# Mixing the next group's preparation into a recurrence: a change of five parts to a chunked RWKV-7 and FFN kernel

## The chip, the cores and the metric

One core of a Trainium2 chip runs the whole kernel. The metric is the device time of one execution in microseconds (us), and less is better. Most executions agree closely; some fall into a slower state with a lower granted TensorE clock. A run that is over 1.5% above the fastest of its kernel is called slow, and fast runs are compared with fast runs only.

Names: PE is TensorE's matmul, PEld its weight load, DVE is VectorE, ACT is ScalarE, POOL is GpSimd, SP is SyncE, which issues most DMAs. L235 is line 235 of the kernel in question, so the same instruction has different lines in different kernels. "Granted" time is time multiplied by the granted clock (1.0 is full, 0.5 half): the full-clock time that TensorE was given.

## The reference

```python
# 4 batches x 8 heads, 768 steps, head_dim 40; all fp32
for t in range(S):
    y[:, :, t] = einsum('bhd,bhde->bhe', rt, state)
    Sa = einsum('bhde,bhe->bhd', state, at)
    state = state * wt[:, :, None, :] - einsum('bhd,bhe->bhde', Sa, bt) \
            + einsum('bhd,bhe->bhde', vt, kt)
x = y.transpose(0, 2, 1, 3).reshape(3072, 320)
h = x @ w_in                        # 320 x 2048, given as float64
g = h * clip(h + 3, 0, 6) / 6
out = g @ w_out                     # 2048 x 320, given as float64
```

The kernel handles the 768 steps in six groups of 128. Within a group the steps become matrix products with a 128x128 lower-triangular system per head. "Preparation" makes all that does not need the state (decay products, scores, the system's blocks); "inversion" inverts the 32x32 diagonal blocks on VectorE; the "recurrence" carries the state through the group and yields 128 tokens per batch; the FFN runs on those tokens. The weights arrive as 64-bit floats, which the kernel takes as pairs of 32-bit words and rounds to fp32 itself, 36 tiles of 128x256 or 128x320.

## The kernel before

`ps_any` gives one of three PSUM banks, `ps_acc` one of two.

```python
def rounded(dst, n, loads):                       # one tile of weights
    raw = tmp.tile([P, DM, 2], U32, name="raw", tag="yg", bufs=2)   # shares yg's slots
    buf = ffn.tile([P, 3, DM], U32, name="parts", tag="gt")
    ...                                           # DMAs on ScalarE's queue; 9 VectorE operations:
    nc.vector.tensor_scalar(x, hi, 20, 0x7FF, ALU.logical_shift_right, ALU.bitwise_and)
    nc.vector.tensor_scalar(e, x, 896.0, 1151.0, ALU.max, ALU.min)
    ...
    nc.gpsimd.tensor_tensor(out=dst, in0=dst, in1=e, op=ALU.add)

def masked(x, s, products):                       # one half (64 rows) of the heads
    o = ps_any([P, 4, P])
    for n, (lhs, rhs) in enumerate(products):     # contraction over 40 rows
        nc.tensor.matmul(out=o[:, n, :], lhsT=lhs, rhs=rhs, start=True, stop=True)
    nc.vector.copy_predicated(out=x[:, 4 * s:4 * s + 4, :], mask=mask4, data=o[:])

def invert(fc):
    ...
    for s in range(1, L):
        nc.vector.tensor_tensor(out=prod, in0=tcol[:, 0:s, 0:s]..., in1=..., op=ALU.mult)
        nc.vector.tensor_reduce(out=tcol[:, s, 0:s], in_=prod, axis=AX.X, op=ALU.add, negate=True)
    ...                                           # then four transposes into tinv

for g in range(NG):                               # the order of a group
    os_ = [prepare(g, q, fc) for q in range(B)]
    invert(fc)
    for q, o in enumerate(os_):
        off_diagonal(q, o)                        # the first to use tinv
    for q, o in enumerate(os_):
        step(q, o)
        outputs(g, q, o, xts[-1])
    if g == 0:
        load_weights()
    else:
        for i, x in enumerate(last):              # FFN of the group before, 256 tokens at a time
            feed_forward(g - 1, i * NB, x)
```

## Time and profile before

The median of four runs was 1623.59 us (1617.91 to 1660.72, the highest one slow). The profiled execution took 1636.3 us at a mean granted clock of 0.742.

| stretch of the kernel before | length, us | granted clock |
|---|---|---|
| preparation 0 | 69 | |
| inversion 0, nothing beside it | 50 | 0.50 |
| recurrence 0, weights, preparation 1 | 197 | 0.59 |
| inversion 1, nothing beside it | 65 | |
| recurrence 1, most of the rounding, preparation 2 | 301 | 0.69 |
| inversion 2 to 5, FFN beside it | 54 each | |
| recurrence and preparation, FFN between | 175, 178, 178 | 0.78 to 0.80 |
| recurrence 5 and the last FFN | 207 | |

A stretch here ends at the first use of an inverse or at the transposes that begin an inversion. From group 2 on the kernel repeats itself every 232 us with TensorE busy; before that it is VectorE's inversions and the weights that hold everything. The prediction below shows and reads the lines of this profile.

### The profile page before, as it was taken

How to read it: one execution, taken by the hardware profiler on the slowest of the kernel's cores; microseconds unless marked ns; L12 is line 12 of the kernel's file. 1: busy time of each engine (PE TensorE's matmuls, PEld its weight loads, DVE VectorE, ACT ScalarE, POOL GpSimd, SP SyncE). 2: the span in 40 equal slices, each digit the busy share in tenths (PEclk: the TensorE clock that was granted, in tenths of full speed). 3: DMA queues.
4: the chain of work that ended last, by engine and by line, in shares of the span. 5: the costliest groups of instructions: out<-in, count | busy, mean ns of one | idle time of the engine just before them, and what ended most of it. 6: DMA issues, size and time to landing. Idle time of an engine off the chain costs nothing.

```text
span 1636.3 us, 21883 instructions
## 1 busy us (share of the span) xinstructions
PE 1360.5 (83%) x8880; PEld 1107.9 (68%) x8880; DVE 775.7 (47%) x1289; ACT 314.3 (19%) x793; POOL 164.4 (10%) x407
## 2 busy tenths in 40 slices
PE   6709987506159999979999989998899999799998
PEld 5608876506048777758877668877577777588765
DVE  6681148897751223691234862245942236912111
ACT  2302112201001112312122221123121123121111
POOL 4100012211110001100011000011000011000000
PEclk6557555556556698788795997786987877876899
DMA  4201022212200012101111101012001121000000
GB/s 63 34 0 22 18 50 57 66 30 55 72 29 18 9 23 41 25 8 22 27 34 29 21 13 25 18 36 41 9 14 22 27 40 25 8 6 8 12 9 12
DMA packets 172949, 44.16 MB, mean 27 GB/s; under 512 B 155952, under 2 KB 168240, under 8 KB 172848
## 3 DMA queue, kind: packets, MB, share of 16 engines
q1 hardware_dynamic: 167184, 32.27, 10.7%
q10 hardware_dynamic: 5664, 10.49, 2.2%
q8 instruction: 70, 1.15, 0.3%
q14 instruction: 31, 0.25, 0.1%
HBM read 34.08 MB, written 3.93 MB: 23 GB/s over the span
## 4 chain that ended last, share of the span: by engine, by line
PE 64%; DVE 27%; ACT 4%; issue 3%; POOL 1%; DMA 0%; ACTq 0%; DVEq 0%; SPq 0%; POOLq 0%
PE h L494 9%; DVE prod L346 8%; PE any L235 8%; PE o L513 7%; PE any L226 7%; DVE tcol L350 6%; PE acc L414 5%; PE acc L407 4%; PE acc L459 4%; PE any L426 4%; PE acc L394 4%; PE any L331 3%; PE h L501 3%; DVE tinv L354 3%; PE any L365 2%
## 5 line engine op out<-in xcount | busy, mean ns | idle before, releaser
L494 PE MATMUL h<-xt,win 128*128 128x256 f32 x768 | 231.9, 453 | 38.5 <-DVE gt L508 30.3
L513 PE MATMUL o<-wout,gt 128*128 128x320 f32 x768 | 232.9, 457 | 10.5 <-DVE gt L508 9.3
L494 PEld LDWEIGHTS h<-xt,win 128*128 128x128 f32 x768 | 166.8, 229 | 75.1 <-DVE gt L508 39.2
L513 PEld LDWEIGHTS o<-wout,gt 128*128 128x128 f32 x768 | 147.8, 198 | 83.9 <-issue 16.5
L236 DVE COPY_PREDICATED score<-mask,any 128x512 f32<-128x512 int32 x144 | 100.5, 722 | 134.5 <-PE any L235 133.9
L508 DVE SCALAR_TENSOR_TENSOR gt<-gt,h 128x512 f32<-128x512 f32 x96 | 63.0, 683 | 175.6 <-ACT gt L506 175.5
L346 DVE TENSOR_TENSOR prod<-tcol,fb 128x1 f32<-128x1 f32 (+30 forms) x186 | 137.1, 737 | 5.0
L432 DVE TENSOR_TENSOR ssum<-any,state 128x160 f32<-128x160 f32 x24 | 7.8, 325 | 273.4 <-PE any L426 273.4
L506 ACT ACTIVATE gt<-h,three 128x512 f32<-128x512 f32 x96 | 61.3, 684 | 243.3 <-PE h L501 242.8
L394 PE MATMUL acc<-state,at 40*128 40x40 f32 x384 | 63.8, 333 | 52.7 <-DVE yg L470 52.7
L501 PE MATMUL h<-xt,win 64*128 64x256 f32 x384 | 75.2, 452 | 29.2 <-POOL win L180 29.2
L394 PEld LDWEIGHTS acc<-state,at 40*128 40x128 f32 x384 | 57.7, 241 | 60.1 <-DVE yg L470 54.5
L365 PE MATMUL any<-tinv,ft 128*96 128x96 f32 x384 | 39.3, 271 | 69.5 <-DVE tinv L354 69.5
L350 DVE TENSOR_REDUCE tcol<-prod 128x1 f32<-128x1 f32 (+30 forms) x186 | 93.5, 502 | 5.0
L414 PEld LDWEIGHTS acc<-U,ft 64*32 64x32 f32 (+2 forms) x1152 | 71.5, 151 | 33.3 <-issue 14.6
L419 ACT ACTIVATE U<-acc 32x320 f32<-32x320 f32 x96 | 41.1, 428 | 273.2 <-PE acc L407 183.5
L235 PE MATMUL any<-at,kt 40*128 40x128 f32 x384 | 75.7, 356 | 19.5 <-ACT ft L320 12.0
L235 PE MATMUL any<-cross 40*128 40x128 f32 x768 | 89.1, 329 | 0.0
L365 PEld LDWEIGHTS any<-tinv,ft 128*96 128x96 f32 x384 | 38.4, 186 | 72.4 <-issue 66.6
L235 PEld LDWEIGHTS any<-cross 40*128 40x128 f32 x768 | 83.8, 227 | 5.2 <-issue 5.2
L331 PEld LDWEIGHTS any<-VN,score 128*128 128x128 f32 x384 | 78.2, 302 | 10.7 <-DVE prod L346 5.5
L414 PE MATMUL acc<-U,ft 64*32 64x40 f32 (+2 forms) x1152 | 82.2, 249 | 3.9 <-ACT U L419 3.9
(101 smaller groups left out, 1899.0 us busy)
## 6 DMA issues: line engine op xcount, KB each, us to landing
raw<-in_moe_w_out_dram ACTq DMA_DIRECT2D x16, 320.0 KB
WN<-in_w_dram SPq DMA_DIRECT2D x24, 160.0 KB
VN<-in_v_dram SPq DMA_DIRECT2D x96, 40.0 KB
AN<-in_a_dram SPq DMA_DIRECT2D x24, 160.0 KB
KN<-in_k_dram SPq DMA_DIRECT2D x24, 160.0 KB
BN<-in_b_dram SPq DMA_DIRECT2D x24, 160.0 KB
RN<-in_r_dram SPq DMA_DIRECT2D x96, 40.0 KB
out_dram<-ob SPq DMA_DIRECT2D x24, 160.0 KB
```

Source lines behind the costliest of these rows:

```text
L226: nc.tensor.transpose(out=o[:, n, :], in_=x[:, 2 * n:2 * n + 2, :].rearrange("p s e -> p (s e)"), identity=ident[:])
L235: nc.tensor.matmul(out=o[:, n, :], lhsT=lhs, rhs=rhs, start=True, stop=True)
L236: nc.vector.copy_predicated(out=x[:, 4 * s:4 * s + 4, :], mask=mask4, data=o[:])
L331: nc.tensor.matmul(out=ev[:, cross(h), :], lhsT=E[:, h % 2 * 4 + h // 2, :], rhs=VN[:, cross(h), 0:D], start=True, stop=True)
L346: nc.vector.tensor_tensor(out=prod, in0=tcol[:, 0:s, 0:s].rearrange("p u t -> p t u"), in1=_ap(fb[:], s * L, [[0, s], [1, s]]), op=ALU.mult,)
L350: nc.vector.tensor_reduce(out=tcol[:, s, 0:s], in_=prod, axis=AX.X, op=ALU.add, negate=True)
L365: nc.tensor.matmul(out=wp[0:LW, pr, :], lhsT=ft[:, 4 * s + pr, :], rhs=tinv[:, q * H + 2 * pr + s, L:P], start=True, stop=True)
L394: nc.tensor.matmul(out=rp[s][:, pr, :], lhsT=o["at"][rows, pr, :], rhs=st[rows, pr, 0:D], start=True, stop=True)
L414: nc.tensor.matmul(out=up[cr, cross(h), :], lhsT=o["F"][0:c * L, h % 2 * 4 + h // 2, (c - 1) * L:c * L], rhs=U[0:c * L, cross(h), 0:D], st ...
L494: nc.tensor.matmul(out=hp[half][:, i, :], lhsT=win[:, kt_, j * P:(j + 1) * P], rhs=xt[:, kt_, :], start=(kt_ == 0 and i == 0), stop=False)
L501: nc.tensor.matmul(out=hp[half][:, i, :], lhsT=win2[rows, (j0 + i) * P:(j0 + i + 1) * P], rhs=xt[rows, 2, :], start=False, stop=(i == 1))
L513: nc.tensor.matmul(out=op[:], lhsT=gt[:, j, i * P:(i + 1) * P], rhs=wout[:, j, :], start=(j == 0), stop=(j == NJ - 1))
```

## The change

The intent has five parts. *Order*: the preparation of group g+1 is issued between the four recurrences of group g, and the FFN of 128 tokens gets the lowest priority ("behind"), to fill what is left. *Row halves paired*: products that use 40 of the 128 rows come alternately from the upper and the lower half of the array, each half with a PSUM bank of its own, so that two can run together. *Inversion in place*: 30 rank-1 updates, two VectorE operations each, without reductions. *Weights*: fewer VectorE operations, two of them moved to GpSimd, and the loads start at once. *FFN by 128 tokens* instead of 256.

```diff
+BEHIND = 1 << 20
 ...
-        buf = ffn.tile([P, 3, DM], U32, name="parts", tag="gt")
+        buf = ffn.tile([P, 3, DM], U32, name="parts", bufs=1)
-            nc.scalar.dma_start(out=raw[rows, 0:n, :],
+            nc.sync.dma_start(out=raw[rows, 0:n, :],
 ...
         nc.vector.tensor_scalar(x, hi, 20, 0x7FF, ALU.logical_shift_right, ALU.bitwise_and)
-        nc.vector.tensor_scalar(e, x, 896.0, 1151.0, ALU.max, ALU.min)
 ...     (eight VectorE operations and one on GpSimd removed; five on VectorE, three on GpSimd now:)
+        nc.gpsimd.tensor_scalar(ef, x, 896.0, 1151.0, ALU.max, ALU.min)
+        nc.vector.tensor_scalar(x, ef, -896.0, 8388608.0, ALU.add, ALU.mult)
         nc.vector.scalar_tensor_tensor(x, hi, 0x80000000, x, ALU.bitwise_and, ALU.bitwise_or)
+        nc.vector.tensor_scalar(m, hi, 0xFFFFF, 0x4B000000, ALU.bitwise_and, ALU.bitwise_or)
+        nc.gpsimd.tensor_scalar(ef, mf, -7.0 * 2 ** 20, 2.0 ** -20, ALU.add, ALU.mult)
+        nc.vector.scalar_tensor_tensor(mf, lo, 2.0 ** -52, ef, ALU.mult, ALU.add)
+        nc.gpsimd.tensor_tensor(out=dst, in0=mf, in1=xf, op=ALU.mult)
 ...
-    def masked(x, s, products):
-        o = ps_any([P, 4, P])
-        for n, (lhs, rhs) in enumerate(products):
-            nc.tensor.matmul(out=o[:, n, :], lhsT=lhs, rhs=rhs, start=True, stop=True)
-        nc.vector.copy_predicated(out=x[:, 4 * s:4 * s + 4, :], mask=mask4, data=o[:])
+    def masked(x, lhs, rhs):
+        o = [ps_any([P, NPR, P]) for _ in range(2)]
+        for n in range(NPR):
+            for s in range(2):
+                rows = slice(SLOT * s, SLOT * s + D)
+                nc.tensor.matmul(out=o[s][:, n, :], lhsT=lhs[rows, n, :], rhs=rhs[rows, n, :],
+                                 start=True, stop=True)
+        for s in range(2):
+            nc.vector.copy_predicated(out=x[:, 4 * s:4 * s + 4, :], mask=mask4, data=o[s][:])
 ...     (the same for at with bt, at with state, and the sums into sn and y)
+        for k in range(1, L - 1):               # inversion in place
+            nc.vector.tensor_tensor(out=pv, in0=_ap(x[:], (k + 1) * L + k, [[L, n], [0, k]]),
+                                    in1=_ap(x[:], k * L, [[0, n], [1, k]]), op=ALU.mult)
+            nc.vector.tensor_tensor(out=rest, in0=rest, in1=pv, op=ALU.add)
 ...
+    os_ = prepared(0)
+    with behind():
+        load_weights()
+    for g in range(NG):
+        def recur(q):
+            step(q, os_[q])
+            xt = outputs(g, q, os_[q])
+            with behind():
+                feed_forward(g, q, xt)
+        if g + 1 < NG:
+            os_ = prepared(g + 1, recur)        # recur(q) ahead of each prepare(g + 1, q)
+        else:
+            for q in range(B):
+                recur(q)
```

## The prediction

> **What bounds the kernel now.** I read the page first, then one period of the steady state cut into its stages, then the longest waits, then instructions in order of time.
>
> ```profile
> PE 1360.5 (83%) x8880; PEld 1107.9 (68%) x8880; DVE 775.7 (47%) x1289; ACT 314.3 (19%) x793; POOL 164.4 (10%) x407
> ...
> PE   6709987506159999979999989998899999799998
> ...
> PEclk6557555556556698788795997786987877876899
> ```
>
> TensorE (PE) is busy in nine tenths or more of most slices from the fourteenth on, at a clock that is granted only in part. Before that are two holes (slice 3, slices 9 to 13). The stretches below are, in columns, start:end and length, busy time of PE, weight load, VectorE, ScalarE and GpSimd with counts, then the granted clock.
>
> ```profile
> 316.00:490.00 174.00, 59.78 (x465) 52.38 (x466) 131.68 (x312) 13.38 (x27) 27.75 (x36) 0.53 0.17 48
> ...
> 912.00:965.00 53.00, 43.20 (x177) 30.55 (x175) 51.03 (x74) 6.38 (x11) 0.00 (x0) 0.90 0.03 9
> 965.00:1063.00 98.00, 97.70 (x920) 81.62 (x922) 21.48 (x43) 20.61 (x42) 6.99 (x24) 0.81 0.11 21
> 1063.00:1144.00 81.00, 75.79 (x388) 62.39 (x385) 36.05 (x44) 24.95 (x79) 13.78 (x36) 0.75 0.21 38
> ```
>
> The last three make one period of 232 us (a group): inversion on VectorE with FFN matmuls beside it, the four recurrences, the next group's preparation. Only in the inversion is VectorE full. The first stretch is group 1 with the rounding of the weights, where VectorE is full and PE a third busy. The waits say the same (who waited for whom, total us, times, longest):
>
> ```profile
> PE any L365 <- DVE tinv L354: 69.5, 6, 44.5
> PE acc L394 <- DVE yg L470: 52.7, 1, 52.7
> ```
>
> L365 waits for an inversion with no FFN to put beside it. L394 stands behind outputs whose yg shares its two slots with the raw weights.
>
> Is PE at its limit in the steady state? I took the time between starts of consecutive matmuls in the trace: at full clock 109 ns for 128 columns with 128 weight columns, 216 for 256, 269 for 320, 112 for 40 columns behind 128 weight columns, 56 for 128 columns in 64-column tiles; at half clock twice that. Counts times these, for the run: FFN h 768 x 216 = 166, its half-row part 384 x 108 = 42, o 768 x 269 = 207: 414 us. The rest: transposes 816 x 109 = 89; K=40 products (L310, L235) 1536 x about 97 = 150; L331, L394, L407 1152 x 112 = 129; L365 384 x 85 = 33; L414 1152 x 36 = 42; L426 768 x 49 = 38; L459 and L466 1152 x 56 = 64: 545 us. In all 959 us of full clock. The mean clock of 0.742 over 1636 us grants 1214. In the recurrence stage (965 to 1063) the work fills what the clock grants; so in the steady state TensorE work and its clock are the bound, and before 490 us it is the weights and inversions.
>
> **What the Trainium skill says.** (1) "TensorE: Matmul & The Clock Gate", Part 1: the clock is either half or full, by recent activity, in windows of about 3.4 us. The trace agrees: only spacings of 109 or 213 ns. Windows that hold mostly transposes and 40-column matmuls are followed by half clock; those that stream FFN by full clock (the end, from 1538 us, is at 1.00). (2) The same page, Part 3: matmuls on different row groups run together. It agrees: half-row matmuls start in pairs 7 ns apart, and eight of them take less than a third of the time of sixteen full ones:
>
> ```profile
> 1572.61 3.72 PE L494 MATMUL h<-xt,win 128*128 128x256 f32 x16 [0.22 <-DVE gt L508]
> 1576.26 1.13 PE L501 MATMUL h<-xt,win 64*128 64x256 f32 x8
> ```
>
> (3) "LDWEIGHTS" in the same page: the load goes by weight columns, 128/1.2 = 107 ns. The 112 ns of 40-column matmuls agree, so an FFN matmul of 128 columns is as long as its weight load. (4) "VectorE: DVE Perf Modes", on the errata: fp32 tensor_tensor takes (N+151)/0.96 ns. The reduce of 961 agrees (1.16 us against 1.158); the product that reads with a stride does not:
>
> ```profile
> 953.56 1.79 DVE L346 TENSOR_TENSOR prod<-tcol,fb 128x961 f32<-128x961 f32 x1
> ...
> 955.85 1.16 DVE L350 TENSOR_REDUCE tcol<-prod 128x31 f32<-128x961 f32 x1
> ...
> 957.51 7.73 DVE L354 STREAM_TRANSPOSE tinv<-tcol 32x1024 f32<-32x1024 f32 x4
> ```
>
> **The change part by part** (PE in us of full clock).
>
> *Row halves paired.* 1536 K=40 products go from about 97 to 56 ns: -63. L394 112 to 58: -21. L426, its halves of columns now alternating, 49 to 29: -15. L466, now four tiles at once, 56 to 28: -11. Sum -110, so 849 remain: 435 recurrent, 414 FFN.
>
> *FFN by 128 tokens.* h becomes 1536 x 109 = 167 instead of 166; o is unchanged; ACT and DVE handle the same 96 tiles of 512. Nothing saved by itself; it gives smaller pieces for gaps, with no slack left for weight loads.
>
> *Inversion.* Two passes of sum k(31-k) = 4960 elements: 9920/0.96 = 10.3 us, plus 60 instructions x 157 ns = 9.4, plus 40 ns between them (as now) 2.4: 22.1. Two transposes of 2.05 us: 4.1. The select about 1.5 and two copies in a row on ACT or POOL about 2.6 (estimates from POOL's 0.40 us for 256 elements and ACT's 0.60 for 512). About 31, with some FFN tiles between 34, against 53.7 now (911.6 to 965.3). VectorE saves about 25 us a group. On the path this counts in full only for the first inversion, which has nothing beside it; later it shortens the stage where PE starves for gt (some 10 us a group).
>
> *Weights.* VectorE per tile of 320: now nine operations, 3.7 us; afterwards 0.33+0.33+0.49+0.32+0.49 = 2.0. Two operations move to POOL. With one parts buffer, tiles stay serial: 2.0 less the 0.32 that overlaps, two POOL operations of about 0.55 (estimate), the last of 0.86, and handovers: about 4.3 us, as now (4.7). So 36 tiles take about 155 us, but can start at the first inversion, not after group 0, and leave VectorE half free.
>
> *Order.* The recurrence of g and preparation of g+1 are mixed and FFN fills gaps. The sum of PE work is the same; its use and clock change. Each change of tile shape costs about 95 ns at full clock (640 changes now); mixing may double them, some +60 us.
>
> The time line: preparation 0 to 64 (68 now, less pairing), inversion to 95. Stage of recurrence 0 and preparation 1: PE work 72 at the clock of such stages (0.58 now) and 85% use: 147 us, to 242; VectorE 55 + 65 of weights fits. Inversion 1 to 276, FFN just begun (12 us of it). Work left: 849 - 28 - 72 - 12 = 737, plus 45 of mode changes beyond those in today's rate: 782. Today's rate in the period is 161/232 = 0.69 (clock 0.82, use 0.85). FFN is now 43% of PE work and becomes 49%, spread: stretches with half FFN show 0.9 now, those with a third 0.75. I take clock 0.88 and use 0.94, 0.83: 942 us, to 1218, and about 10 for the last copy and store: 1228. I chose 1225.
>
> **The rivals.** *Clock stays low.* If small pieces of FFN don't lift the clock (0.75, use 0.92), 782/0.69 = 1133 and 1420. For it: preparation runs at 0.75 with a third FFN. Against: the end at 1.00. *Waits vanish better than thought*, clock 0.95 and use 0.95, few mode changes: 737/0.90 = 819, 1105. *Weights hold up again.* raw still shares slots with yg, and its DMAs now stand in SyncE's queue before the inputs: a hole like 409 to 466 would add 40 to 60: 1275. *VectorE becomes the bound*: per group about 88 us, against 142 of PE: no. *Pairing is done already*: the scheduler pairs some (L310 means 95, not 111), which I counted; if bank waits undo it, +60.
>
> **Range and chances.** Clock and use together from 0.74 to 0.92 give 1340 to 1135; so 1120 to 1335. Slower than 1592 needs a rate below 0.60, worse than today's period with less work: faster 0.96, same 0.03, slower 0.01.
>
> **What would show it.** Right: L365 first near 97; one wait for tinv; first FFN near 255; periods of 170 to 190 us; PEclk mostly 0.8 to 1; L310 and L235 in pairs, with PE's group of L235 halved; the 60 inversion operations near 22 us. Wrong: a hole after 95 longer than 20 us; gt waits; clock of 0.7 in mixed stages; a tail of FFN alone longer than 60 us.

## The result

The change brought 1411.36 us (median of four runs, 1406.3 to 1413.78), against 1623.59 before. Ratios in this document are the mean time of one kernel's fast runs over that of the other's of the same rounds, so they are not quite the ratio of the medians; here 0.8699, with a 95% interval of 0.866 to 0.8738. One hundredth of the ratio is about 16 us. So the kernel became faster, as expected, but 186 us slower than the predicted 1225 and above the top of the range, 1335.

The page of the kernel after, with TensorE's and VectorE's totals, then TensorE's busy tenths and its granted clock in 40 slices of the span:

```profile
span 1411.0 us, 24203 instructions
...
PE 1214.1 (86%) x10032; PEld 1041.7 (74%) x10032; DVE 582.2 (41%) x1113; ACT 327.2 (23%) x805; POOL 248.1 (18%) x503
...
PE   5732725999999998999999999898998999999998
...
PEclk9555656669957899886877759976999989899999
```

TensorE is full from the eighth slice on instead of the thirteenth, and VectorE's busy time fell from 775.7 to 582.2 us. But two holes remain at the start (slices 3 to 4 and 6), and the clock wavers between 0.5 and 0.9 until slice 28. The mean clock rose from 0.742 to 0.805. Span times clock is 1214 granted us before and 1136 after: 78 us less, where the prediction took 110 us of full clock out of the matmuls alone. One caution for every mean clock below: the trace's clock record begins late (at 12 us before, 34 us after), and the profile counts the time until then as full clock, although matmuls of 128 columns start 213 ns apart there, which is half clock. Counted as half, the means are 0.739 and 0.793.

Stretches of the kernel after, in the same columns as the prediction's (start:end and length, then busy time and count of PE, weight load, VectorE, ScalarE, GpSimd, then granted clock and DMA): preparation 0, inversion 0, the stage of recurrence 0 with preparation 1, inversion 1, all that follows, and from it the mixed stage of group 1 and the end.

```profile
0.00:86.00 86.00, 53.25 (x272) 47.23 (x272) 53.15 (x87) 21.81 (x72) 47.40 (x96) 0.72 0.39 74
86.00:131.00 45.00, 3.82 (x16) 3.56 (x16) 38.56 (x105) 2.39 (x3) 22.49 (x29) 0.50 0.17 53
131.00:334.00 203.00, 148.37 (x1262) 130.17 (x1263) 90.24 (x178) 42.62 (x116) 77.20 (x121) 0.66 0.24 53
334.00:366.00 32.00, 27.00 (x186) 22.72 (x185) 25.98 (x67) 6.04 (x10) 3.48 (x4) 0.99 0.03 11
366.00:1411.00 1045.00, 981.70 (x8300) 837.99 (x8299) 374.30 (x678) 254.31 (x606) 97.52 (x255) 0.85 0.12 23
...
366.00:508.00 142.00, 138.16 (x1270) 120.31 (x1270) 53.96 (x79) 42.44 (x115) 21.05 (x60) 0.77 0.21 34
...
1212.00:1405.00 193.00, 179.42 (x1305) 149.16 (x1306) 27.21 (x44) 29.00 (x50) 0.00 (x0) 0.97 0.03 12
```

Here the miss can be split. The prediction's time line has inversion 1 done at 276 and 952 us after it (942 and 10 for the last store). The trace has 366 and 1045. **So 90 us were lost at the start and 93 us afterwards**; together 183, the whole difference to 1228. Two things are to be explained.

What TensorE waited for in the kernel after (who for whom, total us, times, longest):

```profile
PE any L375 <- POOL tinv L367: 46.0, 4, 41.5
PE acc L403 <- DVE yg L479: 44.5, 6, 39.8
```

Both are of the start: 41.5 us for the first inverse, as expected, and one wait of 39.8 us for yg, which was a rival in the prediction. After 366 us nothing like it stands; there the longest wait is a few us, TensorE is busy 981.7 of 1045 us, and mainly the clock and the work are left as explanations.

### The profile page after: what moved, and what is told of

It reads as the page before. It is cut to its first block, busy times and chain, and to the rows that moved or that the text cites. A ratio compares the mean times of both kernels' runs of the same rounds, so it can differ in the third digit from the quotient of the medians.

```text
span 1411.0 us, 24203 instructions
## 1 busy us (share of the span) xinstructions
PE 1214.1 (86%) x10032; PEld 1041.7 (74%) x10032; DVE 582.2 (41%) x1113; ACT 327.2 (23%) x805; POOL 248.1 (18%) x503
## 5 line engine op out<-in xcount | busy, mean ns | idle before, releaser
L528 PE MATMUL o<-wout,gt 128*128 128x320 f32 x768 | 240.4, 462 | 0.0
L505 PE MATMUL h<-xt,win 128*128 128x128 f32 x1536 | 210.8, 296 | 32.9 <-DVE gt L520 32.9
L505 PEld LDWEIGHTS h<-xt,win 128*128 128x128 f32 x1536 | 198.5, 208 | 41.8 <-DVE gt L520 36.3
L332 PE MATMUL any<-VN,score 128*128 128x40 f32 x384 | 78.8, 374 | 9.8 <-DVE score L238 9.8
L332 PEld LDWEIGHTS any<-VN,score 128*128 128x128 f32 x384 | 74.4, 288 | 16.2 <-DVE score L238 11.9
L235 PE MATMUL any<-at,kt 40*128 40x128 f32 x384 | 70.8, 341 | 3.5 <-ACT ft L323 3.5
L403 PE MATMUL acc<-state,at 40*128 40x40 f32 x384 | 31.8, 292 | 44.5 <-DVE yg L479 44.5
L235 PEld LDWEIGHTS any<-at,kt 40*128 40x128 f32 x384 | 62.9, 245 | 7.4 <-ACT ft L323 6.2
L403 PEld LDWEIGHTS acc<-state,at 40*128 40x128 f32 x384 | 28.7, 198 | 50.6 <-DVE yg L479 47.4
L354 DVE TENSOR_TENSOR prod<-x 128x30 f32<-128x30 f32 (+9 forms) x180 | 60.5, 336 | 10.5 <-POOL x L347 5.6
```

Source lines behind the costliest of these rows:

```text
L235: nc.tensor.matmul(out=o[s][:, n, :], lhsT=lhs[rows, n, :], rhs=rhs[rows, n, :], start=True, stop=True)
L332: nc.tensor.matmul(out=ev[:, cross(h), :], lhsT=E[:, h % 2 * 4 + h // 2, :], rhs=VN[:, cross(h), 0:D], start=True, stop=True)
L354: nc.vector.tensor_tensor(out=pv, in0=_ap(x[:], (k + 1) * L + k, [[L, n], [0, k]]), in1=_ap(x[:], k * L, [[0, n], [1, k]]), op=ALU.mult,)
L403: nc.tensor.matmul(out=rp[s][:, pr, :], lhsT=o["at"][rows, pr, :], rhs=st[rows, pr, 0:D], start=True, stop=True)
L505: nc.tensor.matmul(out=hp[half][:, i, :], lhsT=win[:, kt_, j * P:(j + 1) * P], rhs=xt[:, kt_, :], start=(kt_ == 0 and i == 0), stop=False)
L528: nc.tensor.matmul(out=op[:], lhsT=gts[half][:, i, :], rhs=wout[:, half * HJ + j0 + i, :], start=(j0 == 0 and half == 0 and i == 0), stop= ...
```

## The experiments

In the third, fourth and fifth lot many runs of the kernel before fell into the slow state on that chip, and the verdict attached to most ratios there is "unclear"; the ratios below are all of fast runs, with their 95% interval, and kernels of different lots are compared by these ratios, not by their times.

### A. Do the pairs form? forced, unpaired, before_paired

A product in fp32 stands in the trace as two matmuls. When two products run side by side in the two row halves, starts of matmuls are 4 to 7 ns apart. In the kernel after I counted neighbours of one kind at most 10 ns apart among the 1536 matmuls of 40 rows (at most 768 pairs): 0 of 192 for at with kt, 224 of 384 for the scores ("cross"), 32 of 192 for bt with at. That is 256 pairs; the kernel before already had 163. (With neighbours of two kinds, at with kt beside bt with at, it is 299 and 215.) The compiled order shows why the first kind does not pair with itself: in most sets stand four products of one half, then products of the recurrence (L416) or of FFN, then the other half's four. The program order alternates the halves, but it does not bind. The theory: the order in which TensorE gets its instructions is settled by what is ready, the second bank comes later than the first, and so the halves drift apart.

**forced** keeps the pairs together by binding each product behind its predecessor in TensorE's order; nothing else changes, and no semaphore is added.

```diff
+    def in_turn(last, *a, **kw):
+        if last is None:
+            return nc.tensor.matmul(*a, **kw).ins
+        with tc.issue_after(last):
+            return nc.tensor.matmul(*a, **kw).ins
 ...     (in masked, and the same for at with bt)
-                nc.tensor.matmul(out=o[s][:, n, :], ...)
+                last = in_turn(last, out=o[s][:, n, :], ...)
```

> The changed kernel, only the matmuls of the two row halves (the products under the mask and F) are bound to issue in turn, each behind the one before. Theory P (the scheduler undid the pairs because the second half's PSUM bank was not free when it placed them: 112 and 92 ns a matmul where a pair needs 56): means at full clock fall to 56 to 65 ns, 60 us of full clock are saved, time 1340 to 1370. Rival (the banks are really not free on the chip, so PE stands still in order where it now runs the unpaired half): spacing down but waits of PE up by as much, time within 15 us of 1411 or above.

It took 1278.18 us, ratio 0.7863 (0.7779 to 0.7948): 136 us less than the kernel after (0.0836 x 1624). The order of time on TensorE in the kernel after, in group 1, at full clock (start, duration of the whole row, line, tiles, count):

```profile
473.45 1.16 PE L235 MATMUL any<-at,kt 40*128 40x128 f32 x8
```

The same place in forced, also at full clock:

```profile
459.13 1.16 PE L233 MATMUL any<-at,kt 40*128 40x128 f32 x14
```

Eight matmuls fill the time in which fourteen run when paired. The distances between the starts behind the two rows, in ns, read:

```
after:   213 112 112 111 112 112 111
forced:  7 207 6 105 7 105 7 105 6 105 7 105 112
```

Forced has 617 pairs of 768 (661 with neighbours of two kinds). The stretch after inversion 1 and the mixed stage of group 1 in forced:

```profile
343.00:1282.00 939.00, 893.45 (x8280) 749.60 (x8278) 374.98 (x678) 253.58 (x606) 97.28 (x255) 0.92 0.14 26
...
343.00:461.00 118.00, 117.48 (x1333) 99.02 (x1332) 56.05 (x83) 44.85 (x120) 20.90 (x60) 0.99 0.26 43
```

939 us instead of 1045, and the prediction's 952 is met within 1.5%. The mixed stage went from 142 us at a clock of 0.77 to 118 at 0.99. The saving has two shares. With the clocks before rounding, granted time went from 1045 x 0.848 = 886 to 939 x 0.924 = 868, so 18 us of full clock are less work and idling (361 more pairs of 105 ns would be 38). At the old clock that would have saved 18 / 0.848 = 21 of the 106 us; by this reckoning some four fifths are the clock.

**unpaired** is the kernel after with the halves in the old order in all five places.

```diff
-        o = [ps_any([P, NPR, P]) for _ in range(2)]
-        for n in range(NPR):
-            for s in range(2):
+        for s in range(2):
+            o = ps_any([P, NPR, P])
+            for n in range(NPR):
```

> The changed kernel with the order of halves as it was before the change everywhere (products under the mask, F, R, sn, y). Theory P (only R, sn, y and a part of F really paired): costs about 50 us of full clock, 60 us at 0.82, so 1455 to 1485. Rival, as the prediction had it (all pairs taken, 110 us of full clock): 1530 to 1550. If pairs are worth nothing because PE's gaps swallow them: within 15 us of 1411.

Three of its four runs were slow (median 1544.09), so there is no ratio. Its one fast run took 1509.14 us, which is 0.929 of the fast runs of before, or some 96 us above the kernel after. With one run this is weak (and the runs called slow show clocks of 0.751 to 0.775, no clear sign of another state, against 0.769 in the fast one), but the direction is clear: what pairing did survive was worth a good deal. The 96 us lie between the two forecasts and meet neither. For the part of the output with S (L474) and the products with the state (L403) it had survived: 288 and 149 pairs in the kernel after, 0 and 22 in unpaired. Two groups of matmuls, first of the kernel before, then of the kernel after, show the two fates (busy us and mean ns of one stand behind the bar):

```profile
L235 PE MATMUL any<-cross 40*128 40x128 f32 x768 | 89.1, 329 | 0.0
...
L394 PE MATMUL acc<-state,at 40*128 40x40 f32 x384 | 63.8, 333 | 52.7 <-DVE yg L470 52.7
```

```profile
L235 PE MATMUL any<-cross 40*128 40x128 f32 x768 | 89.8, 342 | 2.8 <-DVE score L238 0.7
...
L403 PE MATMUL acc<-state,at 40*128 40x40 f32 x384 | 31.8, 292 | 44.5 <-DVE yg L479 44.5
```

The products with the state halved their busy time; the scores, which the prediction had named as the sign, kept theirs.

**before_paired** gives the kernel before the same pairs, bound in turn as in forced, and nothing else of the change.

```diff
-    def masked(x, s, products):
-        o = ps_any([P, 4, P])
+    def masked(x, lhs, rhs):
+        o = [ps_any([P, NPR, P]) for _ in range(2)]
 ...     (loops and in_turn as in forced, in all five places)
```

> The kernel before, only with the row halves in turn (bound in order, as in the run 'forced'). Work saved at full clock is 95 to 110 us. Theory H (the granted clock follows the share of the array's rows and columns that stream, so two halves at once also lift the clock): mean clock from 0.742 to 0.78 or more, time 1400 to 1460. Rival L (pairs only shorten the list of matmuls): clock within 0.015 of 0.742, time 1480 to 1520 (110 us at 0.8).

It took 1560.23 us, ratio 0.954 (0.9473 to 0.9608), 75 us less. So the pairs pay in the old order too, but both forecasts missed: the saving is smaller than either, and the clock did not rise as theory H says. The profiled run shows 0.772, but its clock record begins only at 64 us; with half clock before that it is 0.751, and the other three runs show 0.748 to 0.756, where fast runs of the kernel before have 0.741 to 0.764.

The stages of recurrence and preparation from group 1 or 2 on say the same by their clock: 0.78 to 0.80 before, 0.77 to 0.78 in before_paired, 0.65 to 0.80 in unpaired, 0.72 to 0.87 after, 0.85 to 1.00 in forced, and 0.77 to 0.81 in forced_plain of part D, which has the pairs without the mixing. Only pairs and mixing together raised the clock. Why the pairs alone do not is left open.

### B. Why does the clock rise? filler, filler_small

The clock moves in windows of 3.41 us. For six traces (before, after, forced, unpaired, raw_own and ffn_mixed; the profiled run of unpaired is called slow) I weighted the streaming time in each window by the share of the array that streams, rows times columns in blocks of 32. Windows followed by a fall from full to half had 0.22 to 0.34 (the middle half of them); windows that stayed full had a median of 0.74. Windows followed by a rise had 0.75 to 0.97, those that stayed at half 0.20 to 0.61. Unweighted busy time tells the falls nearly as well, but not the rises: 0.88 to 1.01 before a rise, 0.29 to 0.90 where the clock stayed at half. A lone product of 40 rows loads two of four row blocks, a pair loads four. If the share of the array is what counts, useless work on the whole array must lift the clock, and the same work on a corner must not.

**filler** puts one useless product of 512 columns with 128x128 weights into the bank of the first half, ahead of each of the 72 sets of products. By its columns that is about 61 us of full clock. **filler_small** does the same on a 32x32 corner.

```diff
         o = [ps_any([P, NPR, P]) for _ in range(2)]
+        nc.tensor.matmul(out=o[0][:]..., lhsT=ident[:], rhs=start[:, 0:NPR * P], ...)                 # filler
+        nc.tensor.matmul(out=o[0][0:L]..., lhsT=ident[0:L, 0:L], rhs=start[0:L, 0:NPR * P], ...)      # filler_small
```

> The changed kernel with one useless full-array product of 512 columns (two instructions of 427 ns at full clock) ahead of each of the 72 groups of products under the mask, into a bank that they then overwrite: 61 us of full clock added, results unchanged. Theory H (clock follows the share of the array in use, which is low in these stages): the mean clock rises by 0.03 or more and the time by less than 35 us. Rival L (work is work): clock as it was within 0.015, time up by 60 to 85 us.

> The run 'filler' with the same 72 useless products of 512 columns, but of 32 rows by 32 weight columns, a sixteenth of the array, for the same time on PE. Theory H (the clock follows the share of the array that streams): no lift, mean clock at most 0.815, time up by 60 to 100 us on 1411 (61 us of full clock at 0.8, plus changes of tile shape). Rival B (the clock follows how long PE streams, whatever the shape): as 'filler', clock 0.84 to 0.86 and time 1390 to 1425.

filler took 1406.33 us, ratio 0.8588 (0.8528 to 0.8648), no more than the kernel after despite its added work; filler_small 1482.58, ratio 0.9029 (0.8945 to 0.9114). They were run at other times. TensorE's totals and clock in filler, then in filler_small:

```profile
PE 1229.0 (87%) x10176; PEld 995.7 (71%) x10176; DVE 580.3 (41%) x1113; ACT 327.3 (23%) x805; POOL 248.0 (18%) x503
...
PEclk9556756779968999898997679968988989999999
```

```profile
PE 1307.0 (88%) x10176; PEld 1045.1 (71%) x10176; DVE 579.4 (39%) x1113; ACT 327.4 (22%) x805; POOL 247.8 (17%) x503
...
PEclk9955557779877798676996579956788968999999
```

The same instructions, the same number of columns, and a mean clock of 0.849 against 0.805 (0.836 against 0.781 with half clock before the record begins). One thing has to be kept apart: by coming first the filler product also changed the order, and both kernels have more pairs than the kernel after (443 and 449 against 256). So that filler costs nothing against the kernel after is not the clock's doing alone. Between the two fillers the pairs are alike, TensorE is as busy, and the changes of tile shape are nearly as many (643 and 667), so that in the main only the share of the array differs: that comparison shows that the clock follows the array's load and not only the time for which it is busy.

### C. Where did 90 us of the start go? raw_own, forced_no_round, raw_forced, raw_forced_late, warm_start

The wait of 39.8 us at 185 to 225 us is read in order of time in the kernel after:

```profile
220.02 0.33 SPq L164 DMA_DIRECT2D raw<-in_moe_w_out_dram  x1
...
220.97 0.33 DVE L169 TENSOR_SCALAR parts<-raw 128x320 uint32<-128x320 uint32 x1 [0.97 <-POOL wout L177]
221.38 1.28 POOL L170 TENSOR_SCALAR parts<-parts 128x320 f32<-128x320 uint32 x1 [0.45 <-DVE parts L169]
222.69 0.33 DVE L171 TENSOR_SCALAR parts<-parts 128x320 uint32<-128x320 f32 x1 [1.16 <-POOL parts L170]
...
224.42 0.76 DVE L479 TENSOR_TENSOR yg<-acc,gam 128x256 f32<-128x256 f32 x2
...
224.90 1.50 PE L403 MATMUL acc<-state,at 40*128 40x40 f32 x9 [39.82 <-DVE yg L479]
```

The two yg operations come between the last weight tiles. yg and raw share two slots, so yg waits until the raw tiles before it have been rounded, one every 4.40 us (221.38 and 225.78 are two starts of L170). The clamp on GpSimd, L170, is 1.28 us of it, with VectorE waiting.

**raw_own** gives raw the four slots of gt, which has no use that early; another tile moved to make room.

```diff
-        raw = tmp.tile([P, DM, 2], U32, name="raw", tag="yg", bufs=2)
+        raw = ffn.tile([P, DM, 2], U32, name="raw", tag="gt", bufs=4)
```

> The changed kernel, only the raw weight tiles no longer share the two slots of yg (they take slots of gt, free until FFN starts). Theory W (the 39.8 us that PE waited for yg at 185 to 225 us is the weights holding its slots, a dead loss): that wait falls under 5 us and the time falls by 30 to 45 us, to 1365 to 1380. Rival (FFN can't start before the last weight anyway, so the recurrence that runs earlier only waits elsewhere): within 12 us of 1411.

It took 1390.63 us, ratio 0.8548 (0.8473 to 0.8623): only about 25 us less. The wait is gone, and the stage of recurrence 0 fell from 203 to 162 us. But with four raw tiles fetched ahead, more rounding gets in front of the start: preparation 0 rose from 86 to 93 us and inversion 0 from 45 to 51.

**forced_no_round** is forced with the rounding taken out: the high word is copied as it is. It measures the price of the rounding wherever it falls. Its output is wrong, which doesn't matter for the time.

```diff
-        (the eight operations of a tile)
+        nc.gpsimd.tensor_copy(dst, hi.bitcast(F32))
```

> The run 'forced' with the rounding of the weights replaced by one GpSimd copy of a word (results wrong on purpose): bounds what the weights' work costs. Theory S (the weights cost the start some 60 to 90 us: preparation and inversion 0 slowed, the wait for yg, FFN late): 1185 to 1225. Rival (FFN catches up later, since PE is full anyway): 1245 to 1280.

It took 1187.26 us, ratio 0.721 (0.7126 to 0.7293), so the rounding costs forced 0.0653, or 106 us. Its stretches are those of the start:

```profile
0.00:69.00 69.00, 45.48 (x271) 40.04 (x272) 41.64 (x45) 21.60 (x72) 31.29 (x84) 0.81 0.55 107
69.00:100.00 31.00, 4.49 (x21) 4.00 (x20) 26.23 (x64) 2.94 (x5) 7.88 (x14) 0.50 0.29 92
100.00:238.00 138.00, 129.89 (x1284) 111.71 (x1285) 53.19 (x79) 42.41 (x115) 27.89 (x75) 0.82 0.32 67
238.00:270.00 32.00, 24.46 (x185) 20.94 (x185) 26.97 (x68) 6.67 (x12) 3.48 (x4) 0.97 0.03 11
```

The prediction's time line was 64, 95, 242, 276; this one is 69, 100, 238, 270. So the times were right for a kernel whose pairs form and whose weights stand in nobody's way, though not their make-up: the stage of recurrence 0 was predicted at a clock of 0.58 without FFN, and it ran at 0.82 with 140 FFN matmuls in it. Of the loss of 90 us, forced gets 23 back by its pairs (inversion 1 ends at 343 instead of 366), and the 73 from there to 270, which is 6 below the predicted 276, are the rounding's: in preparation 0 (VectorE has 87 operations there after, 45 here), in inversion 0 (105 operations against 64) and in the stage behind it.

**raw_forced** joins raw_own's slots to forced. **raw_forced_late** then holds the first four raw tiles back until the first inverse exists, so that no rounding gets in front of it.

```diff
+        if gated[0] < 4:
+            gated[0] += 1
+            nc.gpsimd.tensor_copy(raw[0:1, 0, 0:1].bitcast(F32), tinv[0:1, 0, 0:1])
```

> The run 'forced' with raw tiles in the slots of gt, as in 'raw_own' (which was worth 21 us by itself). If the two parts add up: 1250 to 1265, the wait of R for yg (39 us) gone. If 'forced' has shifted the bound to the weights' chain itself: within 8 us of 1278.

> The same as raw_forced, but the first four weight tiles wait for the first inversion's result, so no weight work stands in the first preparation and inversion. Theory S (weights taken early slow the path to the first recurrence: preparation 0 took 81 to 93 us where 68 were needed, inversion 0 took 45 to 50 where later ones take 32 to 35): L384, the first use of the inverse, starts by 105 us, and the time is 1220 to 1245. Rival G (the weights are themselves what FFN waits for; later weights leave the second inversion and the stage before it without FFN): first FFN later by 20 us or more and time within 12 us of raw_forced, or above it.

raw_forced took 1265.41 us, ratio 0.7723 (0.7649 to 0.7798), 23 us less than forced, so the two parts about add up. raw_forced_late took 1310.85, ratio 0.801 (0.795 to 0.8069), which is slower. Its preparation 0 and inversion 0 were short (71 and 30 us), but the weights were ready so late that inversion 1 had no FFN beside it (54 us instead of 36) and the first output came at 388 us instead of 276. The rounding has to be done somewhere early; moving it back moves the loss back.

**warm_start** asks whether the low clock of that stage is the cause or a sign: two useless full-array products ahead of each set during group 0, on top of raw_forced.

```diff
+        for _ in range(warm[0]):                  # 2 while g == 0, else 0
+            last = in_turn(last, out=o[0][:]..., lhsT=ident[:], rhs=start[:, 0:NPR * P], ...)
```

> raw_forced with two useless full-array products of 512 columns ahead of each group of masked products of preparation 0, recurrence 0 and preparation 1 only (20 groups, 34 us of full clock). Theory H: the clock before the second inversion rises from about 0.7 to 0.85 or more, and that stage (150 us) is 10 to 30 us shorter; time 1235 to 1258. Rival (this stage follows the weights' chain, not PE): within 8 us of 1265, or longer by up to 30.

It took 1292.04 us, ratio 0.7848 (0.7757 to 0.7938), not faster. The stage's clock was 0.84 already in raw_forced and went only to 0.86; its length went from 149 to 161 us, and TensorE was busy 15 us longer in it by the added products. So the run did not bring about what it was to test, and whether this stage follows the clock or the weights' chain, as the rival has it, is not shown by it.

### D. What is the order worth? ffn_mixed, forced_plain

**ffn_mixed** drops "behind": FFN has the priority of what follows it.

```diff
-            with behind():
-                feed_forward(g, q, xt)
+            p = tc.cur_priority
+            feed_forward(g, q, xt)
+            tc.cur_priority = p
```

> The changed kernel, only FFN is not put behind: its instructions get the priorities of those that follow them, so that FFN of one row runs among the next preparation and recurrence. Theory C (the clock of the mixed stages was 0.77 because nearly no FFN stood in them, 17 us of 142, and the FFN left for the end ran at full clock that it did not need): mixed stages rise to 0.85 or more, the tail of FFN alone shrinks from about 190 us to under 60, time down 40 to 90 us, to 1320 to 1370. Rival (FFN keeps the clock up only where it stands in blocks, the rest stays as slow, and the work is the same): mean clock within 0.02 of 0.805 and time within 20 us of 1411.

It took 1513 us, ratio 0.9316 (0.9249 to 0.9383). TensorE's busy tenths and its two longest waits:

```profile
PE   5625609999579999769999769999769999759997
```

```profile
PE any L375 <- POOL tinv L367: 124.1, 6, 41.6
PE h L505 <- DMA xt<-yg: 51.2, 20, 5.4
```

Every inversion is a dip now. The FFN was eaten early, between the recurrences, and the inversions, 31 us each from the second on, had little left beside them (124.1 us of waits instead of 46.0). The second line is a new cost: FFN that follows its outputs at once waits for the DMA that brings yg into xt, 51.2 us in all. The low priority is what keeps FFN in hand for the gaps and gives that DMA time. Pairs are not the reason: 528 form here. With FFN spread, the mixed stages had a clock of 0.80 to 0.83, short of the 0.85 of theory C.

**forced_plain** has forced's pairs, but prepares group g+1 after all four recurrences, as the kernel before did.

```diff
+        for q in range(B):
+            recur(q)
         if g + 1 < NG:
-            os_ = prepared(g + 1, recur)
-        else:
-            for q in range(B):
-                recur(q)
+            os_ = prepared(g + 1)
```

> The run 'forced' with the old order: all four recurrences of a group, then the preparation of the next. As the prediction had it (the sum of PE work is the same, mixing lifts the clock and use): 40 to 100 us slower than 1278, mean clock below 0.86, the stage from one inversion to the next 10 us or more longer. Rival (pairs and FFN behind do it all): within 20 us of 1278.

It took 1424.34 us, ratio 0.8671 (0.8588 to 0.8753), against 0.7863 for forced: the mix is worth about 131 us there, more than the 40 to 100 forecast. A group takes 187 to 195 us in forced_plain, 149 to 167 in forced.

### E. Two other parts alone: before_inv, before_round

**before_inv** is the kernel before with the new inversion alone, **before_round** with the new rounding alone; both edits are those of the change.

```diff
-    for s in range(1, L):  (multiply with strides, reduce)          # before_inv
+    for k in range(1, L - 1):  (multiply, add, in place)
 ...
-    nc.vector.tensor_scalar(e, x, 896.0, 1151.0, ALU.max, ALU.min)  # before_round
+    nc.gpsimd.tensor_scalar(ef, x, 896.0, 1151.0, ALU.max, ALU.min)   (and the rest)
```

> The kernel before with the inversion in place alone. As the prediction had it (inversion 54 to about 34 us, in full only for the first; later about 10 us of starved PE a group): 30 to 70 us less, 1555 to 1595. Rival (all of the 20 us a group are on the path): 115 us or more, below 1515.

> The kernel before with the new rounding of the weights alone. As the prediction had it (a serial chain of about 4.3 us a tile, as before, only VectorE freer): within 20 us of before. Rival (VectorE is what holds the weights up): 45 us or more less. The chain measured in the changed kernel was 4.40 us a tile against 4.72.

before_inv took 1575.94 us, ratio 0.9606 (0.9492 to 0.972), 64 us less. Its inversions went from 50 to 54 us down to 30 to 34, some 20 us each, but the gain was not six times that. From group 2 on a period was 32 + 200 us, and in the kernel before 54 + 178: the same 232. The FFN that no longer fits beside the shorter inversion runs after it. The time was won where nothing stood beside the inversion, in groups 0 and 1 (50 to 30 and 65 to 42), and in the stretch to group 2. before_round took 1641.98 in the median with two of four runs slow; its ratio, 0.986 (0.9721 to 0.9998), is barely a gain.

### F. A better version: two_tiles, two_tiles_dve, best_again, all_dve

**two_tiles** is raw_forced with five slots shared by raw, the scratch of the rounding and gt, so that two weight tiles can be in work at once. **two_tiles_dve** also takes the clamp back to VectorE, and **best_again** is that same kernel with more rounds. **all_dve** takes the second tensor_scalar back as well.

```diff
-        buf = ffn.tile([P, 3, DM], U32, name="parts", bufs=1)                                # two_tiles
+        buf = ffn.tile([P, 2, DM], U32, name="parts", tag="gt", bufs=5)
+        buf2 = ffn.tile([P, DM], U32, name="parts2", tag="ob", bufs=2)
 ...
-        nc.gpsimd.tensor_scalar(ef, x, 896.0, 1151.0, ALU.max, ALU.min)                      # two_tiles_dve
+        nc.vector.tensor_scalar(ef, x, 896.0, 1151.0, ALU.max, ALU.min)
 ...
-        nc.gpsimd.tensor_scalar(ef, mf, -7.0 * 2 ** 20, 2.0 ** -20, ALU.add, ALU.mult)       # all_dve
+        nc.vector.tensor_scalar(ef, mf, -7.0 * 2 ** 20, 2.0 ** -20, ALU.add, ALU.mult)
```

> raw_forced with two weight tiles in work at once (parts in slots of gt, five in all). If the serial chain of 4.4 us a tile (36 tiles, 158 us) is what delays FFN: first output of FFN 40 us earlier than 276, time 1225 to 1250. Rival (the first preparation and inversion get slower by more weight work among their VectorE and GpSimd instructions): within 10 us of 1265.

> The run two_tiles with the clamp of the exponents back on VectorE (0.33 us there, 1.28 on GpSimd). If GpSimd's slow step and the handover hold the weights up: 10 to 30 us below two_tiles. Rival (VectorE is the fuller of the two in these stages, which is why the change moved it away): the same or slower.

> two_tiles_dve once more: median 1230 to 1255, ratio to before 0.745 to 0.765. If the first result was luck of the chip: within 10 us of raw_forced (1265).

> two_tiles_dve with the second tensor_scalar of the rounding on VectorE as well; only the last product stays on GpSimd. If handovers and slow GpSimd steps (0.64 to 0.76 us each plus two handovers of 0.1 to 0.4) hold the weights up: 5 to 20 us below two_tiles_dve. Rival (VectorE now becomes the full one in the first stages): the same within 5 us, or slower.

| kernel | median us | ratio of fast runs (95%) |
|---|---|---|
| two_tiles | 1275.05 | 0.7742 (0.7651 to 0.7832) |
| two_tiles_dve | 1242.16, two of four runs slow | none given |
| best_again | 1243.71, four of seven runs slow | 0.7508 (0.7442 to 0.7575) |
| all_dve | 1254.68 | 0.7658 (0.7622 to 0.7693) |

The second tile alone brought nothing: the clamp on GpSimd is in every tile's chain. With the clamp on VectorE the start was 75 + 37 + 143 + 35 = 290 us in the profiled run of two_tiles_dve (a fast one), against 366 in the kernel after, and the rest 938. The clamp takes 0.35 us in the mean on VectorE (two_tiles_dve) instead of 1.19 on GpSimd (two_tiles). GpSimd seems to carry its share in the best version: with both operations on VectorE the fast runs are slower again, by 0.015 of the ratio. This is weak, because best_again's seven runs spread evenly from 1224 to 1269 us, and over all runs the two differ by 7 us only. best_again beats both kernels of this study. These are the totals and the clock of two_tiles_dve:

```profile
PE 1086.5 (88%) x10032; PEld 917.8 (75%) x10032; DVE 596.4 (49%) x1149; ACT 327.3 (27%) x805; POOL 201.9 (16%) x467
...
PEclk9966976669996899999999997899999699999999
```

## Why the prediction was right or wrong

**"Row halves paired: 1536 K=40 products go from about 97 to 56 ns" failed.** In the kernel after, 256 pairs form of 768, against 163 before; the products of at with kt stay at 112 ns. Between starts of one kind at full clock (gaps over 300 ns left out) the mean is 98 ns before, 89 after and 68 in forced. The prediction counted the loops in the program text and took them for the order on the engine. Its rival "Pairing is done already ... if bank waits undo it, +60" came nearest, though too small, and a wait for banks is not what was found: with the order bound, the same banks let the pairs form. The smaller terms of the same paragraph held: the products with the state measured 61 ns for "112 to 58", the sums into sn 29 to 30 for "29", the part with S 25 for "28". Why the scheduler split the halves (the second bank coming free later) is argued from the compiled order; that the split costs the time is shown by forced. A smaller slip is in a reading: the prediction calls VectorE full in the stretch from 316 to 490, where its own line has 131.68 of 174 us, three quarters.

**"I take clock 0.88 and use 0.94" failed with it.** After inversion 1 the kernel after has a clock of 0.85 and 886 us granted, where the prediction's 942 x 0.88 makes 829. In this order the lone half-array products not only take longer, they let the clock fall: mixed stages at 0.72 to 0.87, against 0.85 to 1.00 in forced. This coupling was not in the prediction, which chose its clock by the share of FFN. With the pairs held, forced needs 939 us for the predicted 952, but at a higher clock (0.92) and with more granted time (868 for 829): two errors that nearly cancel, under a condition that the kernel did not meet. The rival "Clock stays low", 1420, comes within 9 us of the result, but by accident: it has none of the start's loss in it and a clock of 0.75 throughout.

**The time line of the start failed, by its silence on the weights.** "Preparation 0 to 64 ... inversion to 95 ... to 242. Inversion 1 to 276" became 86, 131, 334 and 366. Two terms were mis-sized: the "two POOL operations of about 0.55 (estimate)" measured 1.28 and 0.76 us for 320 elements, and the weights were taken to fit beside the rest because VectorE had time in sum. The tile's chain as a whole was right where it ran alone (about 4.3 predicted, 4.40 measured), but the 36 tiles took from 17 to about 230 us instead of 155 us. What was missing is that early loads put their operations in front of preparation 0 and inversion 0 on the same engine, 42 and 41 extra operations. The rival "Weights hold up again ... a hole ... would add 40 to 60" was right: 39.8 us. That most of the loss, 73 us, is the rounding's is shown by forced_no_round, which keeps the predicted times within 6 us at every step, partly by luck, as said in C; the other 23 are the pairs' again.

**The inversion was right.** Sixty operations took 122.5 / 6 = 20.4 us per group for the predicted 22.1 (with 40 ns between them), and the stage 32 to 36 us for 34. The remark that it counts in full only where nothing stands beside it is what before_inv shows.

**The order was right in kind and is a large part**: 131 us between forced and forced_plain. For the kernel after itself the old order was not run, and the pairs weigh at least as much: forced is some 230 us below the one fast run of unpaired. "Mixing may double" the changes of tile shape was wrong in the pessimistic direction: 575 after, 640 before (653 in forced), so the 45 us set aside for it were not needed.

**FFN "spread" over the groups was wrong in shape.** The prediction named a tail of FFN alone of over 60 us as a sign of error; it is 178 us, from 1230 us on, where the last other matmul ends, and nine of the 24 outputs are computed in it. In itself it costs little, because TensorE is full there and at full clock (1.00). That this FFN, spread over the mixed stages, would have held their clock up is left open: no run here spread it without emptying the inversions (ffn_mixed had 0.80 to 0.83 there).

## What to carry to other kernels

The order in the source is a wish: where two instructions must be neighbours to run together, bind them and count the neighbours in the trace, since busy time and loop nests don't show it. A term of work on TensorE can have a second effect through the clock, which here followed how much of the array streams; price both, and measure them in the order that will run, since the clock was some four fifths of what the pairs were worth in the new order after inversion 1, and nothing measurable in the old one. Work that "fits beside" by sums of busy time still stands in front of something on its engine, so ask, for each early operation, what it is now ahead of.

## What the Trainium skill lacked or had wrong

- "TensorE: Matmul & The Clock Gate", Part 1, says that the clock depends on how busy the engine has been. It lacks that the share of the array counts: the same 72 added products on all of the array gave a mean clock of 0.849, on a 32x32 corner 0.805, with 443 and 449 pairs.
- "GPSIMD Engine Reference", section 4.1 on engine selection, calls operations with one input on GpSimd roughly line-rate against VectorE. A tensor_scalar from uint32 to fp32, mostly at 128x256, measured 1.19 us in the mean on GpSimd (two_tiles) and 0.35 us on VectorE (two_tiles_dve); the fp32 one 0.67 us on GpSimd in the kernel after, 0.31 on VectorE in all_dve.
- "SBUF — State Buffer", section "SBUF: two separate sides", says that an operation of VectorE and one of GpSimd can exclude each other on a shared port pair for the length of the one that came first. The kernel after shows something longer: a first tensor_scalar of VectorE was held for 6.31 us (6.87 to 13.18) while GpSimd ran one memset after another without a gap until 13.03; the same form takes about 0.3 us otherwise. Whether it was this port that held it no run here tested.
- "TensorEngine Tiling (Array Packing)", Key Properties, says that a change of tiling mode drains the engine, without a number. In these traces the next start after a change comes about 95 ns later than usual at full clock and 135 at half (medians over the 575 changes of the kernel after: 94 and 138).
- No page says that pairs of row halves can be lost to the issue order although each half has its own PSUM bank: 256 of 768 formed with the order left to the scheduler, 617 with the order bound.
